# Fewer idle matmuls before an early transpose, and the last output tile copied by one engine

## The chip, the cores and the metric

The kernel runs on one core of a Trainium2 chip. The metric is device microseconds of one execution; the time of the kernel before is the median of three runs. The engines are TensorE (PE, with its weight loads as PEld), VectorE (DVE), ScalarE (ACT), GpSimd (POOL) and SyncE (SP). SyncE issues most of the DMA transfers, ScalarE and GpSimd a few; an engine's own DMA issues are marked with a q (SPq, ACTq).

## What is computed

Linear attention with decay over 768 steps, 4 batches and 8 heads of 48, then a dense layer pair with a piecewise activation:

```python
for t in range(S):                                    # attention, per batch b and head h
    cur = np.einsum('bhd,bhe->bhde', u[None] * kt, vt)
    y[:, :, t] = np.einsum('bhd,bhde->bhe', rt, state + cur)
    state = w[None, :, :, None] * state + np.einsum('bhd,bhe->bhde', kt, vt)
x = np.ascontiguousarray(y.transpose(0, 2, 1, 3)).reshape(B * S, H * D)   # 3072 x 384
h = x @ w_in                                          # 384 -> 2048
g = np.where(h >= 1, h, np.where(h <= -1, 0.0, (h + 1) ** 2 / 4))
return g @ w_out                                      # 2048 -> 384, float32
```

## The kernel before

The 768 steps are cut into 6 chunks of 128, the 4 batches into 2 pairs. A group `g` (0 to 11) is one chunk of one pair; a unit `n` (0 to 23) is one chunk of one batch, two to a group. Within a chunk the attention is done by matmuls, between chunks by a state per batch.

For a group, SyncE loads K, R and v (`load`, `loadV`). K and R are multiplied by tables of the decay (`Ks`, `Rs`, line 325) and transposed: for the first three groups by TensorE with an identity into PSUM (`T`, line 386) and a copy out (`TT`, line 210 through a helper), later by DMA. `V` (line 210) is v in bf16. For a unit, `A` (line 404) is the product of the transposed K and R, which `AT` masks and copies out; `Sp` (line 430) is the unit's addition to the state; `Y` (lines 439 and 444) is its output. The dense layers follow: `mm1` (line 516) into `hp`, three element-wise steps on ScalarE and VectorE (`relu`, `square`, `gate`), `mm2` (line 544) into the PSUM tile `op`, `o`, which copies `op` to SBUF, and `out`, which stores it.

The order of all work is written out by hand in the string `ORDER`; each token is a step with its engine after `@` and its buffer numbers after `:`. No scheduler changes it: each engine runs its own instructions in the order in which the tokens record them, and waits on semaphores for what it needs. A `~9` behind a PSUM step asks for nine matmuls of zeros into the tile before the step writes it (`idle`, line 194, and `psum`, lines 196 to 204); `warm.18` asks for 18 at the start (line 586). Their results are overwritten.

The group 11 is the last. Its two units are copied and stored apart. `o.11.0@D` copies the first of them on VectorE into `o_sb`, and SyncE stores its 192 KB (line 579). `o.11.1@A` finds that `o_sb` exists and takes the branch at line 554: ScalarE copies the left 192 columns, VectorE the right 192, into two tiles `o_last`, and `out.11.1` stores the left from SyncE's queue and the right from ScalarE's (line 577). Both copies read the same PSUM tile.

Of the kernel before, what the change touches and what calls it, by code (L numbers as in the profile page):

```python
# [8 lines left out]
F32 = mybir.dt.float32  # L9
BF16 = mybir.dt.bfloat16  # L10
AF = mybir.ActivationFunctionType
ALU = mybir.AluOpType
AX = mybir.AxisListType

P = 128
# [3 lines left out]
FG = 4  # L19
# [2 lines left out]

TABLES = 2
W_IN = 2
NSPLIT = 2
SPLIT = 2
T_DMA = 3
# [6 lines left out]
warm.18 load.K.0.0:0 load.R.0.0:0 load.K.0.1 load.R.0.1 load.K.1.0:1 load.R.1.0:1 bcu:0 u_bc@D KU.0.0@P:0 RKU.0.0@P:0  # L34
lw loadV.0.0:0 bcw:1 load.K.1.1 KU.0.1@D loadV.0.1 wcol:0 Wdn_p:0 Ks.0.0@D:0 Wup_p load.R.1.1 Rs.0.0@D:0 wCm
KU.1.0@P:1 loadV.1.0:1 Ks.1.0@D:1 warm.4.h.2 T.0:1 load.K.2.0:2 Wdn RKU.1.0@P:1 Rs.1.0@D:1 Rs.0.1@D V.0.0@A:0
RKU.0.1@P T.2:2~9 TT.0@A:0 usum.0.0@D:0 Ks.1.1@D Ks.0.1@D KU.1.1@P Wup Sp.0:0 TT.2@D:1 A.0:1 V.0.1@A load.R.2.0:2
AT.0.1:0 RKU.1.1@P Tm.0@D Sp.1:1~5 T.1:2 Tm.1@D w_in.0 V.1.0@A:1 A.2:1 Rs.1.1@D loadV.1.1 Sp.2:0 AT.0.0 TT.1@D:2
usum.1.0@A:1 A.1:0~8 V2.0.0@P:0 Ks.2.0@P:2 AT.2.0:1 loadV.2.0:0 V2.1.0@A:1 Y.0:1 T.3:2 sbf.0@A Tm.2@D usum.0.1@D Y.2:0
TT.3@D:3 y.2:0 AT.1.1:2 Rs.2.0@P:2 A.3:1~14 X.2:0 V2.0.1@A y.0:1 AT.3.0:3 warm.2.h.2 X.0:1 T.5:2~8 AT.1.0 xT.2@A:0  # L40
# [61 lines left out]
def kernel(  # L102
# [11 lines left out]
    nc = tc.nc  # L114
    B, H, S, D = r.shape
# [3 lines left out]
    DO = moe_w_out.shape[1]  # L119
    nK = DM // P  # L120
    nF = DF // P
# [14 lines left out]
    def flat(x):  # L136
        return x.rearrange("p h d -> p (h d)")
# [23 lines left out]
        out=umask, in_=umask, compare_op=ALU.is_ge, fill=1.0,  # L161
# [22 lines left out]
    Wup = const.tile([P, H, D], F32, name="Wup")  # L184
# [3 lines left out]
    tiles = {}  # L188
# [17 lines left out]
    def buf(i, shape, dtype, name):  # L206
        return work.tile(shape, dtype, name=name, tag=f"{name}{i}")

    def copy(e, out, in_):
        nc.scalar.copy(out, in_) if e == "A" else engines[e].tensor_copy(out, in_)  # L210
# [7 lines left out]
    def span(g, j):  # L218
        return (j, j + 1) if g < NSPLIT else (0, UNITS)

# [65 lines left out]
    def w_in_go(e, bk, i):  # L286
        n = slice(i * DF // W_IN, (i + 1) * DF // W_IN)
        nc.gpsimd.dma_start(out=w_in_sb[:, :, n], in_=w_in_src[:, :, n])

    def w_out_go(e, bk, i):  # L290
        n = slice(i * FG, (i + 1) * FG)
        nc.gpsimd.dma_start(out=w_out_sb[:, n, :], in_=w_out_src[:, n, :])

    do["w_in"], do["w_out"] = w_in_go, w_out_go
# [154 lines left out]
    @step  # L449
    def y(e, bk, n):  # L450
        g, j = divmod(n, UNITS)
        if g < X_DMA:
            t = tiles["y", n] = buf(bk[0], [P, DM], BF16, "y")
        else:
            if j == 0:
                tiles["yy", g] = buf(bk[0], [P, UNITS, DM], BF16, "yy")
            t = tiles["yy", g][:, j, :]
        nc.vector.tensor_add(t, flat(tiles.pop(("Y", n))), flat(tiles["V2", g][:, j * H : (j + 1) * H, :]))  # L458

    @step  # L460
    def Tm(e, bk, n):
# [87 lines left out]
    last = []  # L549

    @step
    def o(e, bk, g, j):
        src = tiles.pop(("op", g, j))
        if g == NCH * BP - 1 and any(key[0] == "o_sb" for key in tiles):

            half = DO // 2
            t = tiles["last", g, j] = [buf(bk[0], [P, half], F32, f"o_last{i}") for i in range(2)]
            nc.scalar.copy(t[0], src[:, :half])
            nc.vector.tensor_copy(t[1], src[:, half:])
            return  # L560
        if g == NCH * BP - 1:
            t = tiles["o_sb", g, j] = buf(bk[0], [P, DO], F32, "o_sb")
        else:
            if j == 0:
                tiles["oo", g] = buf(bk[0], [P, UNITS, DO], F32, "oo")
            t = tiles["oo", g][:, j, :]
        copy(e, t, src)

    def store(e, bk, g, j=None):
        c, bp = divmod(g, BP)  # L570
        rows = out[bp * UNITS * S : (bp + 1) * UNITS * S, :].rearrange("(u s) d -> s u d", u=UNITS)[c * C : (c + 1) * C]
        if j is None:
            nc.sync.dma_start(out=rows, in_=tiles.pop(("oo", g)))
        elif ("last", g, j) in tiles:
            half = DO // 2
            for i, (queue, t) in enumerate(zip((nc.sync, nc.scalar), tiles.pop(("last", g, j)))):
                queue.dma_start(out=rows[:, j, i * half : (i + 1) * half], in_=t)
        else:
            nc.sync.dma_start(out=rows[:, j, :], in_=tiles["o_sb", g, j])

# [47 lines left out]
```

## Time and profile before

| | us |
|---|---|
| median of 3 runs | 175.04 (174.94 to 175.53) |
| the profiled execution | 175.03 |
| its span, first to last instruction | 173.3 |
| TensorE matmuls busy | 163.5 (94%) |
| ScalarE busy | 134.9 (78%) |
| VectorE busy | 134.8 (78%) |
| GpSimd busy | 118.1 (68%) |

The span is what the trace covers; the time of an execution is 1.7 us longer. Rows of the timeline begin with the start and the busy time in us, then engine, line of the kernel, operation, what it writes and reads, its shape and, after x, how many instructions were merged into the row. A bracket at the end tells how long the engine was idle before and what ended that. Matmuls overlap in the pipeline, so the spacing of starts, and not the busy time of a row, gives TensorE's pace.

### The profile page before, as it was taken

To read this page: it belongs to the slowest core of one execution; us is meant where nothing else is said; L and a number is where in the kernel's file an instruction comes from. 1 tells how busy PE (TensorE), PEld (TensorE's weight loads), DVE (VectorE), ACT (ScalarE), POOL (GpSimd) and SP (SyncE) were. 2 spreads that over 40 slices of the span, in tenths; PEclk is the share of its full clock that TensorE was granted. 3 is DMA by queue.
4 is the path that set the end of the run, shared out by engine and by line. 5 is a ranking of instruction groups with operands and counts; after the bars stand their busy time and mean duration, and the time that the engine had idled before them with its cause. 6 is when DMAs were issued, how large, how long until landed. Compare 5 with 4: busy or idle time off the path is not lost.

```text
span 173.3 us, 4141 instructions
## 1 busy us (share of the span) xinstructions
PE 163.5 (94%) x1674; PEld 123.7 (71%) x1674; DVE 134.8 (78%) x168; ACT 134.9 (78%) x194; POOL 118.1 (68%) x96
## 2 busy tenths in 40 slices
PE   7998789998999999979999999999999999999991
PEld 5786578765787866577786868876878868787650
DVE  5699879999987578869978999778996877471472
ACT  4399879977889897169989688998499984988540
POOL 6699999960699999999999699999269300000000
PEclk9999999999999999999999999999999999999999
DMA  5999999999999999999999997999932500402022
GB/s 110 224 223 198 223 185 232 201 173 206 240 175 200 246 159 255 154 186 238 183 235 182 210 213 155 232 229 253 229 77 95 106 2 4 128 8 95 0 91 91
DMA packets 106967, 28.78 MB, mean 166 GB/s; under 512 B 100930, under 2 KB 106180, under 8 KB 106948
## 3 DMA queue, kind: packets, MB, share of 16 engines
q1 hardware_dynamic: 103888, 25.27, 75.2%
q0 software_dynamic: 2912, 3.15, 11.3%
q8 instruction: 13, 0.21, 0.5%
q10 hardware_dynamic: 148, 0.10, 0.2%
q14 instruction: 6, 0.05, 0.1%
HBM read 20.45 MB, written 4.72 MB: 145 GB/s over the span
## 4 chain that ended last, share of the span: by engine, by line
PE 71%; DMA 10%; DVE 9%; ACT 5%; issue 2%; POOL 1%; SPq 1%; DVEq 0%; POOLq 0%
PE hp L516 33%; PE op L544 30%; DMA VF<-in_v_dram 5%; DVE AT L419 3%; DMA xT<-yy 3%; PE A L404 3%; DVE RKU L342 2%; DMA K<-in_k_dram 2%; DVE gt L534 2%; PE Y L444 2%; PE Y L439 2%; PE Sp L430 1%; ACT V L210 1%; ACT RKU L353 1%; POOL V L367 1%
## 5 line engine op out<-in xcount | busy, mean ns | idle before, releaser
L516 PE MATMUL hp<-xT,w_in_sb 128*128 128x256 bf16 (+1 forms) x600 | 70.8, 268 | 2.7 <-DVE gt L534 1.0
L544 PE MATMUL op<-w_out_sb,gt 128*128 128x384 bf16 x384 | 71.7, 326 | 0.0
L534 DVE SCALAR_TENSOR_TENSOR gt<-sq,hp 128x1024 bf16<-128x1024 f32 x48 | 57.9, 1216 | 14.6 <-ACT sq L529 14.3
L516 PEld LDWEIGHTS <-w_in_sb 128*128 128x128 bf16 x600 | 55.8, 98 | 12.8 <-issue 2.9
L524 ACT ACTIVATE pt<-hp 128x1024 f32<-128x1024 f32 x48 | 48.6, 1017 | 13.5 <-PE hp L516 13.3
L529 ACT ACTIVATE sq<-pt 128x1024 f32<-128x1024 f32 x48 | 50.4, 1057 | 3.0 <-DVE gt L534 1.8
L544 PEld LDWEIGHTS <-gt 128*128 128x128 bf16 x384 | 35.6, 98 | 19.7 <-issue 0.2
L419 DVE TENSOR_TENSOR AT<-A,umask 128x1024 bf16<-128x1024 f32 x22 | 26.5, 1218 | 1.8 <-PE A L404 1.5
L367 POOL TENSOR_TENSOR V<-V,diag 128x768 f32<-128x768 bf16 (+1 forms) x12 | 16.5, 1375 | 9.1 <-ACT V L210 7.1
L335 POOL TENSOR_TENSOR KU<-K,u_bc 128x768 f32<-128x768 f32 (+1 forms) x13 | 21.3, 1640 | 1.9 <-DVE u_bc L210 1.8
L342 POOL TENSOR_TENSOR RKU<-R,KU 128x768 f32<-128x768 f32 (+1 forms) x13 | 20.7, 1595 | 0.3
L325 POOL TENSOR_TENSOR Ks<-Wdn,K 128x768 bf16<-128x768 f32 x10 | 18.3, 1828 | 2.1 <-PE Y L444 1.7
L479 POOL TENSOR_TENSOR state<-Tm,wCm 128x384 f32<-128x384 f32 x16 | 16.1, 1008 | 5.1 <-DVE Tm L466 5.1
L325 POOL TENSOR_TENSOR Rs<-Wup,R 128x768 bf16<-128x768 f32 x10 | 18.3, 1830 | 0.0
L458 DVE TENSOR_TENSOR yy<-Y,V 128x384 bf16<-128x384 f32 x18 | 9.9, 553 | 5.0 <-PE Y L444 3.5
L210 ACT CAST V<-VF 128x768 bf16<-128x768 f32 (+1 forms) x14 | 10.2, 736 | 2.7 <-DMA VF<-in_v_dram 2.7
L466 DVE TENSOR_TENSOR Tm<-Sp,state 128x384 f32<-128x384 f32 x16 | 8.9, 553 | 4.3 <-PE Sp L430 3.4
L444 PE MATMUL Y<-V,AT 128*128 128x48 bf16 x192 | 11.2, 184 | 1.1 <-POOL AT L414 0.7
L210 ACT COPY oo<-op 128x384 f32<-128x384 f32 x13 | 6.2, 475 | 7.6 <-PE op L544 7.5
L444 PEld LDWEIGHTS <-AT 128*128 128x128 bf16 x192 | 9.5, 96 | 2.7 <-POOL AT L414 1.0
L355 DVE TENSOR_REDUCE diag<-RKU 128x16 f32<-128x768 f32 (+1 forms) x13 | 11.0, 850 | 0.0
L210 ACT CAST state_bf<-state 128x384 bf16<-128x384 f32 x20 | 10.0, 504 | 0.0
(78 smaller groups left out, 132.0 us busy)
## 6 DMA issues: line engine op xcount, KB each, us to landing
out_dram<-oo SPq DMA_DIRECT2D x11, 384.0 KB, 3.3
K<-in_k_dram SPq DMA_DIRECT2D x10, 384.0 KB, 4.6
R<-in_r_dram SPq DMA_DIRECT2D x10, 384.0 KB, 4.1
VF<-in_v_dram SPq DMA_DIRECT2D x10, 384.0 KB, 5.7
w_in_sb<-in_moe_w_in_dram POOLq DMA_DIRECT2D x2, 768.0 KB, 8.3
w_out_sb<-in_moe_w_out_dram POOLq DMA_DIRECT2D x4, 384.0 KB, 7.4
K<-in_k_dram SPq DMA_DIRECT2D x4, 192.0 KB, 3.7
R<-in_r_dram SPq DMA_DIRECT2D x4, 192.0 KB, 3.7
```

The costliest lines, as they stand in the source:

```text
L210: nc.scalar.copy(out, in_) if e == "A" else engines[e].tensor_copy(out, in_)
L325: engines[e].tensor_mul(of_unit(dst, j0, j1)[:, :, :, :D], rep(tab, j1 - j0), of_unit(tiles[what, g], j0, j1))
L335: engines[e].tensor_mul(of_unit(tiles["KU", g], j0, j1), of_unit(tiles["K", g], j0, j1), rep(u_bc, j1 - j0))
L342: engines[e].tensor_mul(of_unit(tiles["RKU", g], j0, j1), of_unit(tiles["R", g], j0, j1), of_unit(tiles["KU", g], j0, j1))
L367: engines[e].tensor_mul(tiles["V2", g][:, hs, :], tiles["V", g][:, hs, :], tiles["diag", g][:, hs].unsqueeze(2).to_broadcast([P, hs.stop - ...
L419: nc.vector.tensor_mul(t.rearrange("p i n t -> p (i n) t"), tiles.pop(("A", n)).rearrange("p i n t -> p (i n) t"), umask.unsqueeze(1).to_b ...
L444: nc.tensor.matmul(t[:, 2 * p + i, :], tiles["AT", n][:, i, p, :], tiles["V", g][:, j * H + 2 * p + i, :], start=(c == 0), stop=True, skip ...
L516: nc.tensor.matmul(hp[:, f, cols], w_in_sb[:, i, n0 : n0 + P], tiles["xT", g][:, units, i, :], start=(i == 0), stop=(i == nK - 1), skip_gr ...
L524: nc.scalar.activation(tiles["pt", g, q], tiles["hp", g, q], AF.Relu, bias=0.5, scale=0.5)
L529: nc.scalar.activation(tiles["sq", g, q], tiles.pop(("pt", g, q)), AF.Square, bias=0.0)
L534: nc.vector.scalar_tensor_tensor(out=gt, in0=tiles.pop(("sq", g, q)), scalar=1.0, in1=tiles.pop(("hp", g, q)), op0=ALU.min, op1=ALU.max)
L544: nc.tensor.matmul(tiles["op", g, j], tiles["gt", g, q][:, f, j * P : (j + 1) * P], w_out_sb[:, n, :], start=(n == 0), stop=(n == nF - 1),)
```

## The change

Two things differ. In `ORDER`, the transpose step of unit 2 asks for three zero matmuls instead of nine. The last unit's sums are copied by one ScalarE instruction of 384 columns into one tile `o_sb`, and the two stores, on the same two queues, each take a half of that tile's columns.

```diff
-RKU.0.1@P T.2:2~9 TT.0@A:0 ...
+RKU.0.1@P T.2:2~3 TT.0@A:0 ...
...
-            half = DO // 2
-            t = tiles["last", g, j] = [buf(bk[0], [P, half], F32, f"o_last{i}") for i in range(2)]
-            nc.scalar.copy(t[0], src[:, :half])
-            nc.vector.tensor_copy(t[1], src[:, half:])
+            t = tiles["last", g, j] = buf(bk[0], [P, DO], F32, "o_sb")
+            nc.scalar.copy(t, src)
             return
...
             half = DO // 2
-            for i, (queue, t) in enumerate(zip((nc.sync, nc.scalar), tiles.pop(("last", g, j)))):
-                queue.dma_start(out=rows[:, j, i * half : (i + 1) * half], in_=t)
+            t = tiles.pop(("last", g, j))
+            for i, queue in enumerate((nc.sync, nc.scalar)):
+                cols = slice(i * half, (i + 1) * half)
+                queue.dma_start(out=rows[:, j, cols], in_=t[:, cols])
```

The diff also adds two settings that leave this program as it is: `W_OUT = 4` cuts the load of `w_out` into the same four pieces as before, and `FUSE = ()`, a set of groups whose output step would take another form, is empty. On VectorE, GpSimd, ScalarE and SyncE all instructions but those at the end stand as before.

On ScalarE, the end of the program before (`pt` and `sq` are the element-wise steps of the dense layers, `op` the sums in PSUM; the brackets name the semaphores waited for):

```order
L529 ACTIVATE sq_2720<-pt_2714 128x1024 [waits DVE_49,Activation_49]
L524 ACTIVATE pt_2759<-hp_2735 128x1024 [waits PE_49]
L529 ACTIVATE sq_2768<-pt_2759 128x1024 [waits DVE_49,Activation_49]
L558 COPY o_last0_2799<-op_2761 128x192 [waits PE_49]
L577 DMA out_0_dram<-o_last1_2800 128x192 [waits DMAHW4_49,DVE_49]
```

And of the changed program:

```order
L539 ACTIVATE sq_2714<-pt_2708 128x1024 [waits DVE_49,Activation_49]
L534 ACTIVATE pt_2753<-hp_2729 128x1024 [waits PE_49]
L539 ACTIVATE sq_2762<-pt_2753 128x1024 [waits DVE_49,Activation_49]
L567 COPY o_sb_2793<-op_2755 128x384 [waits PE_49]
L587 DMA out_0_dram<-o_sb_2793 128x192 [waits Activation_49]
```

ScalarE's copy has twice the columns, its store waits for that copy and no longer for VectorE, and VectorE's copy (`o_last1<-op`, its last instruction of the program) is gone.

More of the change, by code (lines that the diff above doesn't have):

```diff
@@ L24 @@
 W_IN = 2
+W_OUT = 4
+FUSE = ()
 NSPLIT = 2
@@ L36 @@
 KU.1.0@P:1 loadV.1.0:1 Ks.1.0@D:1 warm.4.h.2 T.0:1 load.K.2.0:2 Wdn RKU.1.0@P:1 Rs.1.0@D:1 Rs.0.1@D V.0.0@A:0
-RKU.0.1@P T.2:2~9 TT.0@A:0 usum.0.0@D:0 Ks.1.1@D Ks.0.1@D KU.1.1@P Wup Sp.0:0 TT.2@D:1 A.0:1 V.0.1@A load.R.2.0:2
+RKU.0.1@P T.2:2~3 TT.0@A:0 usum.0.0@D:0 Ks.1.1@D Ks.0.1@D KU.1.1@P Wup Sp.0:0 TT.2@D:1 A.0:1 V.0.1@A load.R.2.0:2
 AT.0.1:0 RKU.1.1@P Tm.0@D Sp.1:1~5 T.1:2 Tm.1@D w_in.0 V.1.0@A:1 A.2:1 Rs.1.1@D loadV.1.1 Sp.2:0 AT.0.0 TT.1@D:2
@@ L290, in w_out_go @@
     def w_out_go(e, bk, i):
-        n = slice(i * FG, (i + 1) * FG)
+        n = slice(i * nF // W_OUT, (i + 1) * nF // W_OUT)
         nc.gpsimd.dma_start(out=w_out_sb[:, n, :], in_=w_out_src[:, n, :])
@@ L457, in y @@
             t = tiles["yy", g][:, j, :]
-        nc.vector.tensor_add(t, flat(tiles.pop(("Y", n))), flat(tiles["V2", g][:, j * H : (j + 1) * H, :]))
+        Yn = tiles.pop(("Y", n))
+        if g in FUSE:
+            for h in range(H):
+                nc.vector.scalar_tensor_tensor(
+                    out=t[:, h * D : (h + 1) * D], in0=tiles["V", g][:, j * H + h, :],
+                    scalar=tiles["diag", g][:, j * H + h : j * H + h + 1], in1=Yn[:, h, :], op0=ALU.mult, op1=ALU.add,
+                )
+        else:
+            nc.vector.tensor_add(t, flat(Yn), flat(tiles["V2", g][:, j * H : (j + 1) * H, :]))
     @step
```

## The prediction

> **What bounds the kernel now.** I read the head of the page and the chain that ended last, then three stretches of the timeline: the start, where TensorE transposes the first tiles, and the end, where the last sums are copied out and stored.
>
> ```profile
> span 173.3 us, 4141 instructions
> PE 163.5 (94%) x1674; PEld 123.7 (71%) x1674; DVE 134.8 (78%) x168; ACT 134.9 (78%) x194; POOL 118.1 (68%) x96
> PE 71%; DMA 10%; DVE 9%; ACT 5%; issue 2%; POOL 1%; SPq 1%; DVEq 0%; POOLq 0%
> ...
> 13.22 1.81 ACT RKU L353 x16
> 15.04 0.06 ACT V L365
> 15.10 8.50 DMA VF<-in_v_dram
> 23.63 0.84 ACT V L210
> ```
>
> TensorE is busy for 94% of the span and makes 71% of the chain. The diff touches none of the matmuls of the two dense products (lines 516 and 544) that fill it. The last four rows are the chain in order of time at the start (start, us, what): up to 15 us it runs along ScalarE, then through an 8.50 us load of v, which ends at 23.60 us. So what is late or early by a few tenths before 23 us matters only where it moves that load or the work beside it that has no slack.
>
> The two edits lie at the two ends of the program, each beside a chain that this kernel already has. I take them apart, and sum against the profiled execution: 175.03 us for a span of 173.3, so 1.7 us lie outside the span. That execution is 0.01 us from the median of the runs, 175.04. A measurement of this kernel can tell about 0.3%, that is 0.5 us, from no change.
>
> **The start: six zero matmuls fewer.** These are TensorE's rows around the transposes `T.2`, with a column of start and of busy time; the group marked `zeros` at line 202 is the one that shrinks from 9 to 3.
>
> ```profile
> 8.02 0.63 PE L386 MATMUL T<-ident,Ks 128*128 128x128 bf16 x4
> 8.79 0.61 PE L386 MATMUL T<-ident,Rs 128*128 128x128 bf16 x4
> 9.19 1.17 PE L202 MATMUL T<-zeros 128*128 128x128 bf16 x9
> 10.15 0.63 PE L386 MATMUL T<-ident,Ks 128*128 128x128 bf16 x4
> 10.58 0.51 PE L386 MATMUL T<-ident,Rs 128*128 128x128 bf16 x4
> 10.92 0.33 PE L430 MATMUL Sp<-V,Ks 128*128 128x96 bf16 x4
> 11.19 0.40 PE L404 MATMUL A<-TT 48*128 48x128 bf16 x8
> ...
> 18.13 0.61 PE L202 MATMUL T<-zeros 128*128 128x128 bf16 x8
> 18.58 0.39 PE L386 MATMUL T<-ident,Ks 128*128 128x128 bf16 x4
> ```
>
> From 9.19 to 10.15 nine matmuls take 0.96 us, 0.107 each. From 18.13 to 18.58 eight of the same form take 0.45 us, 0.056 each. So TensorE runs at half pace until about 10.7 us and at full pace later. The granted clock of the profile reads 1.00 in both places and doesn't show this; the spacing does. Six matmuls fewer thus free 6 × 0.107 = 0.64 us of TensorE at half pace.
>
> Who uses it? These are the rows of VectorE and ScalarE in the same stretch, which make the inputs of those matmuls and read their results.
>
> ```profile
> 8.65 0.55 DVE L325 TENSOR_TENSOR Ks<-tab,K 128x384 bf16<-128x384 f32 x1
> 9.12 1.01 DVE L325 TENSOR_TENSOR Rs<-tab,R 128x384 bf16<-128x384 f32 x2
> 10.51 1.01 DVE L325 TENSOR_TENSOR Ks<-tab,K 128x384 bf16<-128x384 f32 x2
> 11.43 0.68 DVE L210 COPY TT<-T 128x1024 bf16<-128x1024 bf16 x1
> 9.59 0.50 ACT L210 CAST V<-VF 128x384 bf16<-128x384 f32 x1
> 9.99 1.01 ACT L210 COPY TT<-T 128x1024 bf16<-128x1024 bf16 x1
> 11.37 0.52 ACT L210 CAST V<-VF 128x384 bf16<-128x384 f32 x1
> 11.77 1.03 ACT L410 CAST AT<-A 128x1024 bf16<-128x1024 f32 x1
> ```
>
> Replayed with three zero matmuls: they end at 9.19 + 0.32 = 9.51. `Ks` is ready (8.65 + 0.55 = 9.20), so its transposes run to 9.94; the first of the two `Rs` products is ready by about 9.65 (half of 1.01 after 9.12), so those run to 10.37. `Sp.0` needs the first `V`, ready at 10.09, and takes 4 × 0.08 = 0.32 (three quarters of 0.107 each), to 10.69. `A.0` needs the ScalarE copy `TT.0`, which ends at 11.00. There the gain stops: TensorE now stands idle for about 0.35 us, and `A.0` starts near 11.05 instead of 11.19, 0.14 us earlier. Of the 0.64 us, 0.5 become idle time.
>
> The 0.14 us reach nobody either. `A.0` is read by ScalarE at 11.77, where it comes straight from its row at 11.37 without an idle mark, and `T.2` is read by VectorE at 11.43, straight from the row at 10.51. Both readers are the late side before, so an earlier TensorE only lengthens its own wait. I take 0 for the start. The bounds: a gain of 0.64 us if all of the freed time were passed on, which the idle-free rows speak against; and a loss if the new idle time changes the pace, which is the first rival below.
>
> **The end: one copy, two stores.** The timeline of all engines at the end, and the group row of ScalarE's copy of the same 128x384 shape:
>
> ```profile
> 169.81 0.32 ACT L558 COPY o_last<-op 128x192 f32<-128x192 f32 x1 [3.09 <-PE op L544]
> 170.16 0.36 DVE L559 COPY o_last<-op 128x192 f32<-128x192 f32 x1 [0.44 <-ACT o_last L558]
> 170.19 0.38 SPq L577 DMA_DIRECT2D out_dram<-o_last  x1
> 170.56 0.38 ACTq L577 DMA_DIRECT2D out_dram<-o_last  x1
> ...
> L210 ACT COPY oo<-op 128x384 f32<-128x384 f32 x13 | 6.2, 475 | 7.6 <-PE op L544 7.5
> ```
>
> The half copies don't run side by side: VectorE sat idle for 0.44 us until ScalarE's half was done. They end at 170.16 + 0.36 = 170.52, and the second store is issued at 170.56. One copy by ScalarE takes 0.475 us from 169.81, to 170.29. Issue follows a copy by about 0.05 (170.13 to 170.19), so both stores go out near 170.34: ScalarE's 0.22 us earlier, SyncE's 0.15 us later. Does the end follow the later issue? This is the DMA share of the last stretches (from:to, length, five engines' busy time, PEclk, DMA share, GB/s):
>
> ```profile
> 170.60:170.80 0.20, 0.00 (x0) 0.00 (x0) 0.00 (x0) 0.00 (x0) 0.00 (x0) 1.00 0.92 330
> ...
> 171.20:171.40 0.20, 0.00 (x0) 0.00 (x0) 0.00 (x0) 0.00 (x0) 0.00 (x0) 1.00 1.00 311
> 171.40:171.60 0.20, 0.00 (x0) 0.00 (x0) 0.00 (x0) 0.00 (x0) 0.00 (x0) 1.00 0.97 308
> 171.60:171.80 0.20, 0.00 (x0) 0.00 (x0) 0.00 (x0) 0.00 (x0) 0.00 (x0) 1.00 0.89 284
> 171.80:172.00 0.20, 0.00 (x0) 0.00 (x0) 0.00 (x0) 0.00 (x0) 0.00 (x0) 1.00 0.06 16
> ...
> DMA to landing us min/median/max: 1.7/1.7/1.8
> ```
>
> From 170.6 to 171.8 the 16 DMA engines are at 0.89 to 1.00 of their time with three stores: 192 KB of the other unit, issued at 169.75, and the two halves of 96 KB. That is 384 KB at some 330 GB/s, 1.2 us of work without a hole. The first store sets when it begins, the bytes set when it ends, and the change alters neither. An earlier second half only queues longer. The last landing is now at 170.56 + 1.7 = 172.3, and the span's remaining 1.0 us is the closing of the program, which is not touched.
>
> Three bounds stay. At best the whole 0.22 us is gained (the last landing follows its issue by 1.7 as now). By the shares, about 0.05 us is to be had, the holes in 1.2 us. At worst the two issues hinder each other now that they fall together; the nearest row for that is the start, where both queues issue at once:
>
> ```profile
> 0.80 0.55 ACTq L150 DMA_DIRECT2D w_row<-in_w_dram  x1
> 0.81 0.46 SPq L302 DMA_DIRECT2D K<-in_k_dram  x1
> ```
>
> They took 0.55 and 0.46 there against 0.38 here: up to 0.17 us later, and with the later SyncE half as much as 0.15 + 0.17 = 0.3 for the first half store, of which the busy engines hide what lies before 171.2. I take 0 for the end, from −0.22 to +0.2, nearest to the row that shows full engines.
>
> On this place the Trainium skill (DMA: Bandwidth & Descriptors, "Issuing engines are not separate DMA queues") says that transfers issued from different engines run on the same 16 DMA engines and interleave, so a second queue saves issuing time only. The shares of 0.89 to 1.00 agree, and by that rule too the end moves by nothing.
>
> VectorE loses its last copy, and nothing is queued behind it. SyncE's half store now waits for a copy 0.16 us longer; only the closing of the program is queued behind it.
>
> The sum: 175.03 + 0 + 0 = 175.0 us.
>
> **The rivals.** *TensorE keeps its half pace longer (slower).* The six matmuls keep TensorE busy just before the pace changes at about 10.7 us. With them gone it idles from 10.69 to 11.05. If the pace depends on how busy TensorE has been, the change may come later. For this: the four matmuls at 8.02 end at 8.45, a hole of 0.34 us before the next at 8.79, and the full pace came only after 8.79 to 10.7 without a hole. Against: the hole is small, and the replay leaves TensorE busy up to 10.69, nearly the moment of the change. The price, from the rows of that stretch:
>
> ```profile
> 10.92:15.05 4.13, 3.54 (x61) 2.70 (x58) 4.13 (x8) 4.13 (x22) 4.02 (x6) 1.00 1.21 226
> ...
> 15.05 0.37 PE L444 MATMUL Y<-V,AT 128*128 128x48 bf16 x8 [0.49 <-POOL AT L414]
> ...
> ACT V L210 <- DMA VF<-in_v_dram: 1.6, 2, 1.1
> ```
>
> Some 61 matmuls lie in 10.92 to 15.05 (second column), each 0.05 dearer at half pace: 3.1 us if the pace stays low throughout, some 1.5 if for half of it. Of that 0.49 goes into TensorE's wait at 15.05. VectorE, ScalarE and GpSimd are busy for 4.02 to 4.13 of the 4.13 us, so what TensorE hands them late makes them late too; ScalarE's later wait of 1.1 us for the load of v takes some of it back. From 0 to 2 us remain; I take 0.7, half of the stretch and part of the waits: 175.7 us. It decides once `A.0` ends after 11.88, when ScalarE is free to read it.
>
> The Trainium skill (TensorE: Matmul & The Clock Gate, "Part 1: The HAM clock gate") puts this as a rule: the array's clock is gated to half until TensorE has been busy for a window of about 3.4 us, which runs freely. Its spacings for 128 columns, 107 and 56 ns, agree with 0.107 and 0.056 above; no row of this profile shows the window. By that rule a failed window would cost an estimated 3.4 us more of half pace, 1.7 us of TensorE before waits.
>
> *The freed time is passed on (faster).* If readers of `T.2` and `A.0` or the order of loads behind them gain the 0.64 us, the result is 174.4 us; with the best end, 174.2. For it speaks that TensorE is the bound over the whole span; against it that VectorE and ScalarE have no idle mark before those reads, and the 8.50 us load behind them.
>
> *The end is worse by the issue together.* 0.2 to 0.3 us, 175.3 at most; within 0.3%.
>
> That the change does not do what it says is excluded: the copies and stores are written as told, and the six matmuls leave the order.
>
> **How the numbers follow.** Nothing that shows: 0.60, with the small gains and losses at the end in it. The slow pace: 0.24, nearly all beyond +0.5 us. The freed time passed on: 0.16, beyond −0.5. Likeliest is 175.0. The forecast's own range is 174.7 to 175.5: the end by −0.22 or +0.3, and the start by −0.14. To leave out no more than 2 in 10 I reach into both other cases: down to 174.4, where the freed time is passed on, and up to 175.9, which takes in the rival's 175.7 but not its 177.
>
> **What would show it.** In the changed profile, the transposes of `T.2` should start near 9.5 us, `A.0` near 11.05 with an idle mark on TensorE until ScalarE's `TT`, and the ScalarE copy at 11.77 and the load of v's end at 23.6 should stand where they do. Spacings near 0.107 after 11.5 us would show the first rival. At the end, one copy of about 0.48 us, two issues within 0.1 us of each other, and DMA shares near 1 up to 171.8 on the same scale. The prediction is wrong if the load of v, or the first matmuls of line 516, move by more than 0.5 us, or if the last landing does.

## The result and the profile after

The changed kernel takes 174.21 us (median of 4 runs, 173.92 to 174.47) beside 175.17 of before (174.94 to 175.53): a ratio of 0.9946, 95% interval 0.9923 to 0.9969. That is 0.96 us faster, 0.2 us below the range. All ratios here leave out the executions of a slower state that comes up now and then, while the medians in us of the experiments keep them, so a ratio isn't quite that of the two medians beside it.

The head of the page of the profile after, which answers to that of before:

```profile
span 172.4 us, 4127 instructions
PE 163.6 (95%) x1668; PEld 123.6 (72%) x1668; DVE 133.6 (78%) x167; ACT 135.4 (79%) x194; POOL 118.2 (69%) x96
PE 73%; DMA 7%; DVE 6%; POOL 5%; SPq 4%; ACT 2%; issue 1%; DVEq 0%; POOLq 0%
```

The span is 0.9 us shorter with the same busy time of TensorE (163.5 and 163.6); the DMA part of the chain fell from 10% to 7%. The start came out nearly as replayed (TensorE and ScalarE, profile after):

```profile
9.38 0.63 PE L388 MATMUL T<-ident,Ks 128*128 128x128 bf16 x4
10.93 0.61 PE L406 MATMUL A<-TT 48*128 48x128 bf16 x8 [0.17 <-ACT TT L212]
11.71 1.01 ACT L412 CAST AT<-A 128x1024 bf16<-128x1024 f32 x1
```

The transposes of `T.2` start at 9.38 (9.5 foreseen), `A.0` at 10.93 behind ScalarE's copy with an idle mark (11.05), and ScalarE's next copy at 11.71 beside 11.77 before. The cast of v that waits for the 8.50 us load starts at 23.45 beside 23.63. The first matmul of line 516 starts at 21.46 before and 21.39 after, and a later one, the first of the loop that then runs on, at 30.82 and 30.76: next to nothing was won up to there.

The end, profile after, is also as foreseen:

```profile
168.68 0.34 SPq L589 DMA_DIRECT2D out_dram<-o_sb  x1
168.74 0.48 ACT L567 COPY o_sb<-op 128x384 f32<-128x384 f32 x1 [3.09 <-PE op L554]
169.25 0.35 SPq L587 DMA_DIRECT2D out_dram<-o_sb  x1
169.25 0.38 ACTq L587 DMA_DIRECT2D out_dram<-o_sb  x1
```

The DMA share behind it (the column next to the last):

```profile
169.60:169.80 0.20, 0.00 (x0) 0.00 (x0) 0.00 (x0) 0.00 (x0) 0.00 (x0) 1.00 1.01 369
170.40:170.60 0.20, 0.00 (x0) 0.00 (x0) 0.00 (x0) 0.00 (x0) 0.00 (x0) 1.00 1.02 315
```

One copy of 0.48 us, both stores issued at 169.25, the DMA engines full. From the end of the last matmul to the end of the span it is 3.67 us, against 3.55 before: 0.1 us lost, not won.

The time came from the middle, 70 us into the span, where neither edit lies. SyncE's queue of before and of after, then TensorE's rows of both (before: line 516; after: line 526):

```profile
70.02 1.21 SPq L501 DMA_TRANSPOSE xT<-yy  x1
71.34 2.54 SPq L396 DMA_TRANSPOSE KT<-Ks  x1
...
72.84 0.81 PE L544 MATMUL op<-w_out_sb,gt 128*128 128x384 bf16 x4
74.63 1.03 PE L516 MATMUL hp<-xT,w_in_sb 128*128 128x256 bf16 x8 [0.98 <-DMA xT<-yy]
```

```profile
69.94 1.21 SPq L511 DMA_TRANSPOSE xT<-yy  x1
71.26 1.24 SPq L398 DMA_TRANSPOSE KT<-Ks  x1
...
72.75 0.81 PE L554 MATMUL op<-w_out_sb,gt 128*128 128x384 bf16 x4
73.40 1.36 PE L526 MATMUL hp<-xT,w_in_sb 128*128 128x256 bf16 x11
```

The DMA transpose `xT` of the group's attention output is issued at the same time in both, 70.02 and 69.94. Before, it lands 4.57 us later and TensorE stands idle for 0.98 us; after, it lands in 2.7 us and TensorE goes on without a gap, 1.23 us earlier. The lead is 1.07 us a few microseconds later and stays 1.07 to the last matmul. The DMA engines in those microseconds, before and then after (columns as at the end of the prediction's tables: length, five engines, PEclk, DMA share, GB/s):

```profile
72.00:72.50 0.50, 0.50 (x5) 0.29 (x3) 0.45 (x1) 0.00 (x0) 0.50 (x2) 1.00 0.49 94
72.50:73.00 0.50, 0.50 (x8) 0.37 (x6) 0.00 (x0) 0.00 (x0) 0.50 (x1) 1.00 3.95 127
73.00:73.50 0.50, 0.50 (x5) 0.29 (x3) 0.46 (x1) 0.00 (x0) 0.50 (x1) 1.00 0.03 3
73.50:74.00 0.50, 0.15 (x1) 0.00 (x0) 0.50 (x2) 0.31 (x1) 0.35 (x2) 1.00 0.09 9
```

```profile
72.00:72.50 0.50, 0.50 (x5) 0.31 (x4) 0.36 (x1) 0.00 (x0) 0.50 (x2) 1.00 0.19 36
72.50:73.00 0.50, 0.50 (x8) 0.37 (x7) 0.05 (x1) 0.00 (x0) 0.50 (x1) 1.00 1.14 263
73.00:73.50 0.50, 0.50 (x5) 0.31 (x4) 0.50 (x2) 0.00 (x0) 0.45 (x1) 1.00 1.15 256
```

Before, transfers that are under way move next to nothing for a microsecond (3 and 9 GB/s from 73.0 to 74.0). The share of 3.95 just ahead is that of packets which began there and took more than a microsecond each: 21 packets of 256 bytes with a mean of 1.32 us, where most of that size take 0.02. All 21 end together, between 74.11 and 74.16. After, there is no such hole.

One more thing lies in the DMA record at that place. A program is itself read by DMA, on a queue of its own; the row of that queue on the page is the same in both profiles (packets, MB, share of the 16 engines):

```profile
q8 instruction: 13, 0.21, 0.5%
```

In a narrow window the row shows when one such read runs; this is before, 72.0 to 73.3 us, where after has no such row:

```profile
q8 instruction: 1, 0.02, 6.5%
```

Thirteen reads of 16 KB in the whole span. The row doesn't say whose program it is; I take it for TensorE's, because before the reads come 253 rows of TensorE's apart in the mean (184 to 367), and ScalarE, which comes next on the page, has 194 instructions in all. In every profile below, the read near 72 us begins when TensorE has run 1453 to 1487 rows of its program. Before, it runs from 72.00 to 73.36, after from 73.58.

Twelve TensorE instructions fewer, six weight loads and six matmuls, put everything behind them twelve places earlier against these reads. That is only a part of the shift of 1.58 us. The read began when TensorE had run 1453 rows before and 1469 after; after reached 1453 rows at 72.63, so the twelve places make some 0.6 us. Why the read began sixteen rows later in the count besides is not known.

### The profile page after: what moved, and what is told of

Same layout as the page of the kernel before. It is cut to its first block, busy times and chain, and to the rows that moved or that the text cites. A ratio compares the mean times of both kernels' runs of the same rounds, so it can differ in the third digit from the quotient of the medians.

```text
span 172.4 us, 4127 instructions
## 1 busy us (share of the span) xinstructions
PE 163.6 (95%) x1668; PEld 123.6 (72%) x1668; DVE 133.6 (78%) x167; ACT 135.4 (79%) x194; POOL 118.2 (69%) x96
## 4 chain that ended last, share of the span: by engine, by line
PE 73%; DMA 7%; DVE 6%; POOL 5%; SPq 4%; ACT 2%; issue 1%; DVEq 0%; POOLq 0%
PE op L554 32%; PE hp L526 32%; DMA w_in_sb<-in_moe_w_in_dram 5%; SPq L304 4%; PE A L406 3%; DVE RKU L344 2%; DMA R<-in_r_dram 2%; DVE AT L421 2%; PE Y L446 2%; PE Y L441 2%; DVE gt L544 2%; PE Sp L432 1%; POOL AT L416 1%; POOL Rs L327 1%; POOL Ks L327 1%
## 5 line engine op out<-in xcount | busy, mean ns | idle before, releaser
L554 PE MATMUL op<-w_out_sb,gt 128*128 128x384 bf16 x384 | 71.8, 326 | 0.1
```

The costliest lines, as they stand in the source:

```text
L554: nc.tensor.matmul(tiles["op", g, j], tiles["gt", g, q][:, f, j * P : (j + 1) * P], w_out_sb[:, n, :], start=(n == 0), stop=(n == nF - 1),)
```

## The experiments

**Theory F.** The read of TensorE's instructions at 72 us stalls the DMA transpose that is under way, and taking out twelve instructions moved the read behind the end of the transpose. **Rival E:** the gain is the new end. **Rival S:** it is the earlier `T.2` and `A.0`. **Rival G,** in the second set: it is the smaller number of zero matmuls as such.

The first four runs take the change apart and move twelve instructions elsewhere.

**The zero matmuls alone.**

```diff
 # the kernel before
-RKU.0.1@P T.2:2~9 TT.0@A:0 ...
+RKU.0.1@P T.2:2~3 TT.0@A:0 ...
```

> The kernel before with three zero matmuls ahead of T.2 instead of nine, and its old end. Theory F (fetch): the 12 PE instructions fewer (6 weight loads, 6 matmuls) move the 16 KB instruction fetch that lay at 72.0 us, inside the DMA transpose of xT issued at 70.0, to about 73.6 us, after its end, and xT lands 1.9 us earlier: 174.1 to 174.3 us beside 175.2 before, about -1.0 us. Rival E (end): the gain is the one copy and the earlier second store: no change here, 175.2. Rival S (start): T.2 and A.0 earlier give the gain: -1.0 us here too.

Measured: 174.86 us beside 175.45, ratio 0.9956 (0.9937 to 0.9976), a gain of 0.8 us where 1.0 was expected. The read lies at 74.05, `xT` lands in 3.1 us. The gain belongs to this edit; rival E is out.

**The end alone.** The changed kernel with `T.2:2~9`.

> The changed kernel with nine zero matmuls ahead of T.2, so only the end is new. Theory F: 175.2 to 175.3 us, no change or 0.1 us slower (the traces show 3.65 us from the last matmul's end to the span's end against 3.54 before), fetch near 72 us inside the transpose of xT. Rival E: the whole gain, 174.2. Rival S: no change.

Measured: 175.49 beside 175.45, ratio 1.0004 (0.9985 to 1.0023), the read at 72.50 and `xT` late again. From its chain:

```profile
70.14 4.45 DMA xT<-yy
```

The last matmul's end to the span's end took 3.65 us, as after. The end costs 0.1 us in every profile that has it (3.65 to 3.67 against 3.53 to 3.56 with the old one), too little for the times to show.

**Six other zero matmuls, 9 us later.**

```diff
 # the kernel before
-TT.3@D:3 ... warm.2.h.2 X.0:1 T.5:2~8 AT.1.0 xT.2@A:0
+TT.3@D:3 ... warm.2.h.2 X.0:1 T.5:2~2 AT.1.0 xT.2@A:0
```

> The kernel before with nine zero matmuls ahead of T.2 as they were, and six fewer ahead of T.5 (two instead of eight), at 18.1 us, where TensorE waits 0.40 us for GpSimd at 19.37 anyway. Theory F: every later PE instruction stands 12 places earlier as in the changed kernel, the fetch comes near 73.6 us, 174.1 to 174.3 us. Rival S: the start up to 18 us is that of before, so no change, 175.2. Rival E: no change, 175.2.

Measured: 174.63 beside 175.45, ratio 0.9949 (0.9918 to 0.9981), the read at 74.12, `xT` in 3.5 us. `T.2` stood as before and `A.0` 0.3 us later (11.48), and the gain came all the same: rival S is out.

**The six put back at that other place.** The changed kernel with `T.5:2~14`.

> The changed kernel (three zero matmuls ahead of T.2, one copy at the end) with six more ahead of T.5 (fourteen instead of eight), which puts every later PE instruction back to its place of before. The six take 6 x 0.056 = 0.33 us, inside the wait of 0.40 at 19.37. Theory F: the fetch is back near 72 us, 175.1 to 175.3 us, the gain is gone. Rivals S and E: the gain stays, 174.2 to 174.3.

Measured: 175.87 beside 175.45, ratio 1.0029 (1.0016 to 1.0041). The read is back at 72.80, and TensorE's row shows the wait again:

```profile
75.26 1.47 PE L526 MATMUL hp<-xT,w_in_sb 128*128 128x256 bf16 x12 [1.30 <-DMA xT<-yy]
```

So the changed kernel loses its gain by six zero matmuls at a place where TensorE waits anyway. It came out 0.6 us above the 175.1 to 175.3 expected. Of that 0.25 lies in before itself (175.45 in this experiment, 175.2 in the expectation); besides, `xT` lands 4.9 us after its issue, 0.3 more than before, and it was issued 0.3 us later (70.34).

These four fit theory F, but in the two that gain against before, work was taken out. The next runs move the read by other amounts and in the other direction.

**Twelve more instead of fewer.**

```diff
 # the kernel before
-TT.3@D:3 ... A.3:1~14 ... T.5:2~8 AT.1.0 xT.2@A:0
+TT.3@D:3 ... A.3:1~20 ... T.5:2~14 AT.1.0 xT.2@A:0
```

> The kernel before with twelve zero matmuls MORE: six ahead of A.3 (twenty instead of fourteen) and six ahead of T.5 (fourteen instead of eight), 0.67 us more work for TensorE at 0.056 each, of which the waits of 0.26 at 17.49 and 0.40 at 19.37 hide most. Theory F: every later PE instruction stands 24 places later, so the fetch that lay at 72.0 comes about 3 us earlier, near 69 us, before the packets of the xT transpose (from 71.0). xT lands in 2.7 us, and a kernel with more work is faster than before: 0.993 to 0.998 of its time, less 1.0 us and up to 0.3 us for the added work. Theory G: the gain comes from fewer zero matmuls as such, not from the fetch's place: no change or up to 0.4 us slower, 1.000 to 1.002.

Measured: 174.40 beside 175.57, ratio 0.9939 (0.9918 to 0.9960). A kernel with more work is faster, and rival G is out. But the profiled execution was, at 175.05, the slowest of the ten: there the read began at 71.30 and not near 69, and `xT` took 4.5 us. The size of the shift in time was mis-guessed; where the read lay in the executions around the median, this profile doesn't tell.

**Six more.** The kernel before with `T.5:2~14`.

> The kernel before with six zero matmuls more ahead of T.5 (fourteen instead of eight), 0.34 us that the wait of 0.40 at 19.37 hides. Theory F: the fetch comes at 70.4 to 71.0 us and lasts to about 72, over the first packets of the xT transpose; if any overlap stalls it, 1.000 to 1.002; if only the late overlap does, 0.994 to 0.996. Theory G: 1.000 to 1.002.

Measured: 175.31 beside 175.57, ratio 0.9975 (0.9948 to 1.0001), inconclusive: nine of its ten executions spread from 174.52 to 175.68. In the profiled one (175.66) the read began at 72.96, not earlier than before, and `xT` took 5.0 us. The reads don't move strictly with the count.

**Three fewer.** The kernel before with `T.5:2~5`.

> The kernel before with three zero matmuls fewer ahead of T.5 (five instead of eight). Theory F: six PE instructions fewer, the fetch comes near 72.9 us, at the very end of the xT transpose (72.7 when nothing stalls it): either still stalled (0.999 to 1.001) or free (0.994 to 0.996), and which of the two follows from where its fetch lies: free if it begins after xT has landed. Theory G: half of the gain, 0.997 to 0.998.

Measured: 174.76 beside 175.57, ratio 0.9953 (0.9921 to 0.9985): the whole gain for half of the edit rather than half, though 0.997 lies within the interval. Its profiled execution was late from the start (the first matmul of line 516 at 25.56 us, 21.46 before), so the place of its read can't be set beside the others.

**Twelve fewer.** The changed kernel with `T.5:2~2`.

> The changed kernel with six zero matmuls fewer ahead of T.5 too (two instead of eight), twelve fewer than before in all. Theory F: the fetch comes near 75 us, after the xT transpose has landed: the same gain as the changed kernel's and no second one at this place, 0.994 to 0.996 of before; other fetches move too and may cost or give some tenths. Theory G: twice the gain, 0.989 to 0.991.

Measured: 174.79 beside 175.57, ratio 0.9965 (0.9935 to 0.9995). No second gain: the read at 74.83, `xT` in 2.7 us. Once the read is out of the way, moving it further brings nothing.

**Six put back, but behind the place.**

```diff
 # the changed kernel
-gate.4.0:7 y.11 A.12:0 xT.10:2 ...
+gate.4.0:7 y.11 A.12:0~6 xT.10:2 ...
```

> The changed kernel with six zero matmuls put back, but ahead of A.12, after the xT transpose of 70 us (some 0.34 us of TensorE, which is nearly without idle time there). As much work as in the run that had its six back ahead of T.5 and was 1.0029 of before. Theory F: the fetch of about 73.6 us keeps its place because no instruction ahead of it moves, xT lands in 2.7 us, and only the work costs: 0.996 to 0.998 of before. If the number of instructions mattered and not the place of the fetch: 1.002 to 1.004.

Measured: 174.92 beside 175.58, ratio 0.9968 (0.9947 to 0.9989), as expected and not as the run with six put back ahead of it (1.0029). The read at 74.75, 3.67 us after the issue of `xT` at 71.08, which landed in 2.8 us. The same number of instructions, on the other side of the read, leaves most of the gain.

**Twelve more, a second profile.** The same kernel as above.

> The same kernel as the run with twelve zero matmuls more, whose median was 0.9939 of before while its profiled execution was the slowest of its ten, with the fetch at 71.30 us and xT late. A second profile. Theory F: where the execution takes 174.0 to 174.5 us, the fetch lies before about 71 us or after 73 us and xT lands within 3.5 us; where it takes 175 us, the fetch lies between and xT lands after 4.5 us. An execution at 174.2 with xT landing after 4.5 us would speak against it.

Measured: 174.67 beside 175.58, ratio 0.9940 (0.9903 to 0.9977). Again the profiled execution lay far above the median (175.35, in a spread from 174.37 to 175.43), with the read at 71.63 and `xT` in 4.4 us. That agrees with the theory but again shows only the case with the late transpose.

**Eighteen more.** The kernel before with `A.3:1~26` and `T.5:2~14`.

> The kernel before with eighteen zero matmuls more: twelve ahead of A.3 (twenty-six instead of fourteen) and six ahead of T.5 (fourteen instead of eight), 1.0 us of TensorE, of which the waits of 0.26 at 17.49 and 0.40 at 19.37 hide most. Every later PE instruction stands 36 places later, 12 more than in the two runs with twelve more, whose profiled executions still had the fetch at 71.3 and 71.6 us. Theory F: the fetch comes near 70 us on this scale, at or before the issue of the xT transpose, xT lands within 3.0 us of its issue in the profiled execution too, and the time is 0.994 to 0.998 of before although TensorE has more work. Theory G (number of instructions or work): 1.002 to 1.006.

Measured: 174.76 beside 175.70, ratio 0.9943 (0.9924 to 0.9962). The granted clock of its profile is 1.00 up to 96 us and 0.93 from there to 120 us; it is read up to 80 us only. The read begins at 70.31; its queue's row in the window from 70.2 to 70.6 us:

```profile
q8 instruction: 1, 0.02, 18.4%
```

And TensorE's row of the timeline has no wait in front:

```profile
73.14 1.47 PE L516 MATMUL hp<-xT,w_in_sb 128*128 128x256 bf16 x12
```

`xT`, issued at 69.67, landed in 3.4 us (3.0 or less was expected; its issue alone took 2.28 instead of 1.21), and line 516 went on at 73.14, 1.5 us earlier than before, behind 1.0 us of added matmuls.

All profiled executions but that of three fewer, in order of where the read begins, counted from the issue of `xT`:

| kernel | read begins after the issue, us | xT lands after, us |
|---|---|---|
| eighteen more | 0.64 | 3.4 |
| twelve more, second | 1.16 | 4.4 |
| twelve more | 1.20 | 4.5 |
| before | 1.98 | 4.6 |
| the end alone | 2.36 | 4.5 |
| the six put back | 2.46 | 4.9 |
| six more | 2.71 | 5.0 |
| after | 3.64 | 2.7 |
| six put back behind | 3.67 | 2.8 |
| zero matmuls alone | 3.70 | 3.1 |
| twelve fewer | 4.42 | 2.7 |
| six other | 4.43 | 3.5 |

Reads that begin 1.2 to 2.7 us after the issue go with 4.4 to 5.0 us, those that begin 3.6 us or more after it, when the transpose has landed, with 2.7 to 3.5. With eighteen more the read began before the first packet of the transpose (70.84) and ended 0.65 us behind it; 19 packets of 256 bytes were held there too, but for 0.8 us in the mean, and it landed in 3.4.

## Why the prediction was wrong

**The step that failed** is "I take 0 for the start", and with it the list of what six zero matmuls do. It counted their time on TensorE and the readers of the next results. It did not count that each is also two places in TensorE's program, and that everything behind it, up to the end, moves against the reads of that program. The term was missing; in this pair of profiles it is worth 1.1 us, the lead of 1.07 that begins where `xT` lands on time. The sentence that the diff touches none of the matmuls that fill the span was true of their work and not of their place.

**The start, right.** The freed 0.64 us became idle time: `A.0` waited for ScalarE's copy, ScalarE read it 0.06 us earlier than before, and the first matmul of line 516 moved by 0.07 us.

**The end, right within its bounds.** The copies, the issues and the full DMA engines came as worked out. The size was 0.1 us on the wrong side of 0, inside −0.22 to +0.2. In the profile before, the row that mattered was VectorE's wait of 0.44 for ScalarE's half; the Trainium skill (PSUM — Partial Sum Buffer, "PSUM bank collisions raise a hardware error") tells that two engines must not read one PSUM bank at once and that a semaphore has to keep them apart. That row agrees: the two half copies, which read the same tile, ran one behind the other.

**Half pace for longer, right that it can come and wrong on its price.** After the change the full pace came at about 12.8 us:

```profile
12.30 0.63 PE L388 MATMUL T<-ident,Ks 128*128 128x128 bf16 x4
12.72 0.44 PE L388 MATMUL T<-ident,Rs 128*128 128x128 bf16 x4
13.10 0.40 PE L406 MATMUL A<-TT 48*128 48x128 bf16 x8
13.53 0.33 PE L432 MATMUL Sp<-V,Ks 128*128 128x96 bf16 x4
```

Four matmuls from 12.30 to 12.72 are 0.105 us apart, eight from 13.10 to 13.53 are 0.054. That is 2 us later than in the profile before. Whether the edit did it isn't shown: the moment varies between profiles of the same front, from 10.8 to 13.7 us with nine zero matmuls and from 11.7 to 15.3 with three. Two microseconds more of half pace cost nothing that is left at 21.4 us; I had priced the rival at 0.7, and the waits ahead of line 516 take it. Where the full pace came at 15.2 and 15.3 us (the six put back at either place), line 516 began at 21.86 and 22.62, and in the others (three fewer aside) at 21.3 to 22.0, so a longer delay may cost some tenths; no run separates that.

**The freed time passed on,** at 174.4 or 174.2, has the measured size by chance. No profile shows it: the lead at 30.8 us is 0.06.

The rows that would have warned were in the profile of before: the chain's piece at 70 us, and the row of the nine transposes of its kind with their median time to landing:

```profile
70.02 4.57 DMA xT<-yy
```

```profile
xT<-yy SPq DMA_TRANSPOSE x9, 2.8
```

One transfer 1.8 us over its median, with TensorE waiting for it. I read the chain only where the diff lies.

**What stays open.** Shown is that the same six matmuls, put back ahead of the read or behind it, take the gain away or leave most of it (1.0029 and 0.9968), that taking out twelve instructions and putting in 24 or 36 both bring a gain, and that in twelve profiles the late transposes are those with a read that begins 1.2 to 2.7 us after their issue. The packet records tie the stall to the read more closely still: in each of the six late profiles the 18 to 21 held packets end together, within 0.05 us of one another, 0.8 to 0.9 us after the read's end, which itself lies anywhere from 72.97 to 74.33.

How one read of 16 KB holds up all of them is not shown to the end. The Trainium skill (DMA: Bandwidth & Descriptors, "Queues, rings and completion order") says that a DMA engine changes between queues only at the end of a packet. The read is one packet of 16,384 bytes and 1.36 us, so by that rule one engine of sixteen is closed to the transpose for that long. The trace agrees in that the stall comes with the read, and what runs in the 0.8 us behind the read looks like that one engine catching up: 3 or 4 packets in each 0.1 us, in all six profiles, where before the read all sixteen engines moved 335 in 0.4 us (71.4 to 71.8), some 5 for each engine in 0.1 us. That the others wait until it has caught up is an inference; the records don't name the engine.

Three things speak against too simple a rule. Packets are also held where no program is read: before, 16 packets of 256 bytes near 38 us took 1.30 us in the mean, with the nearest reads at 34.76 and 47.60 and GpSimd's load of `w_out` under way, and all profiles have such a group there. The reads don't move strictly with the count of instructions (the run with six more). And the kernel with twelve more was never caught in a profile at a time near its median, so that its gain comes from the same place is not shown.

No version that was run beats the changed kernel clearly: the zero matmuls alone, with the old end that is 0.1 us shorter by the traces, came out at 0.9956, the changed kernel at 0.9946, with intervals that overlap.

## What to carry to other kernels

An edit of a few instructions on an engine with thousands can move every later instruction of it against the reads of its program, as here, so a gain or loss that shows far from the edit should first be looked for in the transfers that are late there. Before a small edit is judged by its time, put the same number of instructions in or out at a harmless place: if the time changes as much, the gain wasn't the edit's own. In the profile, transfers of one kind whose time to landing is well above their median, with an engine waiting behind them, are where such luck is lying.

## What the runs showed of the hardware

What I take for TensorE's program is read in thirteen DMA packets of 16 KB on the transfers' own engines, each 0.9 to 1.9 us long in these profiles. Where one began 1.2 to 2.7 us after the issue of the transpose `xT`, some 20 packets of 256 bytes took 1.1 to 1.8 us in the mean instead of 0.02, next to nothing moved until 0.8 us after the read's end, and the transpose landed 4.4 to 5.0 us after its issue instead of 2.7 to 3.5. Not each overlap holds packets: after the change, a read from 109.85 to 111.02 ran beside 107 transpose packets, none of which took over 0.05 us.
